# The order of emission of a fused attention and feed-forward kernel, rewritten from the thirtieth microsecond on

## The chip, the core and the metric

The kernel runs on one core of a Trainium2 chip. The metric is the device time of one execution in microseconds. Times of engines and waits come from one profiled execution. The five engines are TensorE (PE; PEld is its weight load), VectorE (DVE), ScalarE (ACT), GpSimd (POOL) and SyncE (SP), which here issues most DMAs. Each engine works through its own instructions in the order in which the program emitted them, and waits at the head of its queue until what the instruction needs is there.

## The reference

```python
# x (8, 8, 512, 64), state (8, 8, 32, 64): batch, head, token, depth
scores = x @ state.T / sqrt(D);   xread = softmax(scores) @ state      # tokens read the states
scores2 = state @ x.T / sqrt(D);  sread = softmax(scores2) @ x         # states read the tokens
x = concatenate([xread, sread], axis=2), heads side by side            # (8, 544, 512)
h = maximum(x @ w_in, 0)                                               # 512 -> 1024
conv_out = sum over k of conv_w[k] * h shifted by k - 1 along the tokens
out = (h * sigmoid(conv_out)) @ w_out                                  # 1024 -> 512
```

Everything is float32.

## The kernel before

The eight batches are taken one after the other, and the 1024 columns of the middle layer in eight slices of 128. A batch and a slice make a step `i = 8 b + f`, 64 steps in all. The 512 tokens of a batch lie on the free axis in a step; the 32 state tokens of four batches at a time are a side job of eight slices each (`ss`, `gts`, `acc_t` in the names).

Before its steps a batch needs the attention: `scores` on TensorE, softmax both ways on ScalarE and VectorE (`top`, `exp2`, `flip`, `read` for the states; `att_flip` to `att_low` for the tokens), and `state_product`, which multiplies the states by `w_in` at once, so that the first layer of a step is attention weights `a` times `u`. Products that must be exact to float32 are made of three passes of a high and a low part (`PASSES`): a value is split by `high` on ScalarE (L205) and `low` on VectorE (L208).

One step is this chain: `hidden` (six matmuls into `ps_h`, L630), `relu` (ScalarE L200 or VectorE L202, into `h`), `middle` (the middle tap, ScalarE L194 or VectorE L196, into `t`), `before` and `behind` (the other two taps, VectorE L673 and L678), `sigmoid` (a tanh on ScalarE, L682), `gate` (VectorE L687), `gate_high` (ScalarE L205, `g0`), `gate_low` (VectorE L208, `g1`), and then four times `project` (three matmuls each, L705), one for each 128 tokens, which add the slice to one of four accumulators `acc`. After eight steps `end` (L719, L721) copies an accumulator out of PSUM and `store` writes it. `join` and `edge` (GpSimd, L648) copy one column each between `h` and the state tokens' `hs`: `behind` reads what `join` has written, and the side job what `edge` has.

Weights arrive as `raw` and are rounded and split first (`w_abs` to `w_low`; `whole` and `wo` are `w_out`'s). Buffers are few: eight PSUM banks, five of `h`, five of `t`, four of `g0` and of `g1`, one of `xx` (the tokens for `read`), four of `xt`.

All operations are first entered in a list with what they read and write, in program order; `Plan.order` then emits them in the order of the numbers in `ORDER`. A number with a `v` puts the operation on VectorE instead of ScalarE, and `-n` emits n idle matmuls. Nothing else sets the order. It may be any that respects the reads and writes:

```python
        for word in ORDER.split():
            i = int(word.rstrip("v"))
            ...
            assert after[i] <= done and i not in done, "an operation before one that it needs"
            fns.append(partial(self.ops[i][2], on=self.vector) if word[-1] == "v" else self.ops[i][2])
```

Of the kernel before, what the change touches and what calls it, by code (L numbers as in the profile page):

```python
# [61 lines left out]
199 191 43 515 490 44 535 491 45 47 193 46 202 203 48 205 516 493 204 517 49 536 206 502 503 210 504 519v 494 537 520  # L62
# [12 lines left out]
228 662 607 611 229 639 706 691 690 656 623 638 1661 721 676v 663 654 707 677 664 665 424 678 666 340 425 719 689 692  # L75
# [14 lines left out]
447 938 448 967 1027 1030 482 473 953 1029 980 474 483 485 997 400 401 1045v 402 1031 475 968 476 484 941 999 1015 478  # L90
# [6 lines left out]
1068 1139 1124 1080 1140 1173v 1094 1108 1067 1070 1095 1174 1081 1096 1157 1109 1083 1143 1082 374 1172 1097 1171  # L97
1142 1141 1069 1175 1176 1089 1110 1085 1098 1100 1111 1159 1125 375 377 1084 1112 1144 376 378 1126 1104 1156 1116
1160 1161 1128 1177 409 1129 1199 1184 1117 1543 991 1145 1200 1185 1130 1544 1186 1187 1127 1545 1178 1131 1546 1132
1548 1133 1099 1214 1229 1549 1188v 1162 1550 1230v 1134 1114 1120 1163 1146 1551 1121 1552 1539 1215 1553 1113 1115  # L100
1118 1547 1252 1216 1189 1147 1164 1554 1122v 415 418 1148 416 417 1137 1149 1218 1297 1135 1282 1150 1179 449 1556
1557 1136 1165 419 1558 1219 1233v 1253v 1190 1220 1123 1119 1256 1203 1204 1231 1201 1191 1217 1152 1555 1167 1182
1151 1221 1192 1138 1180 1193 1559 1298v 1234 1235 1202 1232 1254 1194 1257 1205 1258 1560 1561 1236 1206 1153 1312
1301v 1168 1166 1181 1222 1562 1237 1207 1267 1195 1183 1313v 1197 1198 1259 1208 1563 1342 1223 1209 1210 1224 1283
1302 1299 1255 1564 1268 1271 1238 1565 1566 1272 1269 1273 1213 1239 1274 1212 1227 1225 1567 1568 1275 1569 1196
1211 1285 1300 1284 1570 1286 1270 1343v 1346v 1572 1287 1573 1347 1574 1288 1228 1226 1241 1243 1575 1240 1289 1246
1260 1250v 1576 1357 450 1327 1242 1358v 1577 1578 1303 1276 1261 1304 1571 1579 451 1247 452 1262 1277 1290 456 1328v
1316v 1248v 1249 453 454 1265 1291 455 1305 1263 1306 1280 1585 1251 1380 1381 459 1315 1580 1345 1383 457 1382 1344
1317 1307 1292 1278 1384v 1586 1244 1314 1245 1385 1587 1361 460 1318 1331 1359 1319 1362 1363 1320 1266 1295 1264
1410 1281 1293 1364 1386 1411 1588 1589 1348 1365 1321 1590 1591 1279 1296 1308 1294 1322 458 1311 1395 1387 1388 1332  # L110
1396 1326 1397 1329 1330 1593 1366 1398 1309 1399v 1470 1594 1323 1455 1310 1349 1350 1595 1596 1333 1597 1456v 1413
1334 1335 1425 1598 1351 1599 1352 1601 1602 1400 1592 1485 1324 1600 1426 1427 1457 1336 1428 1360 1337 1603 1401
1458 1412 1604 1605 1471 1402 1606 1607 1609 1610 1459v 1414 1440 1341 1339 1325 1611 1612 1415 1367 1416 1613 1614
# [5 lines left out]
1479 1376v 1377 1453 1468 1469 1452 1645 1480 1646 1647 1648 1494 1649 1650 1373 1652 1651 1495 1467 1483 1484 1466  # L119
1482 1497 1653 1499 1506 1507 1514 1515 1504v 1505 1512 1513 1498 1510 1508 1511 1509 1481 1496 1500 1502 1501 1503  # L120
"""


class Plan:

# [825 lines left out]
```

## Time and profile before

| | |
|---|---|
| three runs | 356.61 us median, 355.37 to 356.98 |
| span of the profiled execution | 354.1 us, 2.5 under the median of the runs |
| TensorE | 348.6 us, 98%; weight loads 271.8 us, 77% |
| VectorE | 316.1 us, 89% |
| ScalarE | 256.1 us, 72% |
| GpSimd | 29.4 us, 8% |
| chain that ended last | 97% on TensorE |
| read from HBM, written | 25.71 MB, 8.91 MB |

A busy share is an average over the whole span: the windows say where an engine has room. The chain that ended last is followed back from the last instruction; each step of it goes to what released an instruction, or to the one before it on its engine. A chain that lies on one engine nearly all the time says that this engine was waited for, and did not wait. Durations of one instruction overlap those of the next one on the same engine, so starts tell more than sums of durations.

### The profile page before, as it was taken

To read this page: it belongs to the slowest core of one execution; us is meant where nothing else is said; L and a number is where in the kernel's file an instruction comes from. 1 tells how busy PE (TensorE), PEld (TensorE's weight loads), DVE (VectorE), ACT (ScalarE), POOL (GpSimd) and SP (SyncE) were. 2 spreads that over 40 slices of the span, in tenths; PEclk is the share of its full clock that TensorE was granted. 3 is DMA by queue.
4 is the path that set the end of the run, shared out by engine and by line. 5 is a ranking of instruction groups with operands and counts; after the bars stand their busy time and mean duration, and the time that the engine had idled before them with its cause. 6 is when DMAs were issued, how large, how long until landed. Compare 5 with 4: busy or idle time off the path is not lost.

```text
span 354.1 us, 6694 instructions
## 1 busy us (share of the span) xinstructions
PE 348.6 (98%) x2538; PEld 271.8 (77%) x2538; DVE 316.1 (89%) x563; ACT 256.1 (72%) x560; POOL 29.4 (8%) x90
## 2 busy tenths in 40 slices
PE   7999999999999999999999999999999999999995
PEld 6766758876788868878789887878788868888884
DVE  1999999999999999999999999987799898889950
ACT  3999999998777997859856657774745447548642
POOL 1000000010000000100000300042201001113000
PEclk9999999999999999999999999999999999999999
DMA  7989998201600033030400000001200011000205
GB/s 255 396 309 377 328 357 302 62 1 50 219 0 2 0 127 142 3 119 32 180 30 2 0 31 31 30 3 60 89 2 0 0 71 65 2 2 0 74 33 176
DMA packets 13584, 35.06 MB, mean 99 GB/s; under 512 B 1520, under 2 KB 4720, under 8 KB 12528
## 3 DMA queue, kind: packets, MB, share of 16 engines
q1 hardware_dynamic: 12976, 34.28, 27.1%
q8 instruction: 20, 0.33, 0.4%
q10 hardware_dynamic: 576, 0.35, 0.3%
q14 instruction: 12, 0.10, 0.1%
HBM read 25.71 MB, written 8.91 MB: 98 GB/s over the span
## 4 chain that ended last, share of the span: by engine, by line
PE 97%; DMA 2%; ACT 0%; SPq 0%; issue 0%
PE acc L705 47%; PE ps_h L630 22%; PE ps_h L637 4%; PE ps_hs L615 4%; PE ps_u L548 4%; PE acc_t L705 3%; PE ps_r L368 2%; PE ps_t L355 2%; PE ps_s L310 2%; DMA xt<-xT 2%; PE acc_c L705 2%; PE acc L713 2%; PE ps_u L567 1%; PE ps_s L498 1%; PE ps_x L498 1%; PE ps_x L512 1%
## 5 line engine op out<-in xcount | busy, mean ns | idle before, releaser
L705 PE MATMUL acc<-wo,g 128*128 128x512 f32 x726 | 177.0, 393 | 0.0
L705 PEld LDWEIGHTS acc<-wo,g 128*128 128x128 f32 x726 | 134.7, 188 | 32.8 <-issue 1.7
L630 PE MATMUL ps_h<-a,u 128*128 128x512 f32 x336 | 83.2, 391 | 0.0
L630 PEld LDWEIGHTS ps_h<-a,u 128*128 128x128 f32 x336 | 62.7, 188 | 13.1
L682 ACT ACTIVATE t<-t 128x512 f32<-128x512 f32 x64 | 39.9, 630 | 14.5 <-DVE t L678 14.3
L673 DVE SCALAR_TENSOR_TENSOR t<-h,cw,t 128x511 f32<-128x511 f32 x64 | 47.1, 742 | 1.6 <-ACT t L194 1.5
L678 DVE SCALAR_TENSOR_TENSOR t<-h,cw,t 128x512 f32<-128x512 f32 (+1 forms) x64 | 46.8, 745 | 0.6
L205 ACT ACTIVATE g<-t 128x512 fp32r<-128x512 f32 (+1 forms) x62 | 37.5, 615 | 11.0 <-DVE t L687 5.5
L687 DVE SCALAR_TENSOR_TENSOR t<-t,h 128x512 f32<-128x512 f32 (+1 forms) x64 | 42.4, 667 | 2.3 <-ACT t L682 2.2
L208 DVE TENSOR_TENSOR g<-t,g 128x512 fp32r<-128x512 f32 (+1 forms) x62 | 41.3, 671 | 3.5 <-ACT g L205 3.1
L194 ACT ACTIVATE t<-h,cw 128x512 f32<-128x512 f32 x52 | 36.9, 723 | 4.3 <-DVE h L202 3.0
L200 ACT ACTIVATE h<-ps_h 128x512 f32<-128x512 f32 x56 | 33.3, 596 | 9.3 <-PE ps_h L630 6.1
L648 POOL COPY h<-hs 128x1 f32<-128x1 f32 x40 | 14.2, 376 | 129.2 <-ACT sr L383 66.3
L205 ACT ACTIVATE u<-ps_u 128x512 fp32r<-128x512 f32 x28 | 16.2, 596 | 8.5 <-PE ps_u L548 8.5
L719 ACT ACTIVATE o<-acc 128x512 f32<-128x512 f32 (+1 forms) x30 | 15.8, 544 | 8.5 <-PE acc L705 8.3
L648 POOL COPY hs<-h 128x1 f32<-128x1 f32 x40 | 13.6, 361 | 97.6 <-ACT h L200 80.9
L208 DVE TENSOR_TENSOR u<-ps_u,u 128x512 fp32r<-128x512 f32 x28 | 18.6, 682 | 2.5 <-ACT u L205 2.5
L615 PEld LDWEIGHTS ps_hs<-sr,wi 128*128 128x128 f32 x128 | 14.8, 192 | 1.1 <-ACT t L194 0.8
L637 PE MATMUL ps_h<-p,u 128*128 128x256 f32 x64 | 15.3, 386 | 0.0
L615 PE MATMUL ps_hs<-sr,wi 128*128 128x128 f32 x128 | 15.0, 276 | 0.0
L548 PE MATMUL ps_u<-wi,st 64*32 64x512 f32 x224 | 14.3, 597 | 0.0
L637 PEld LDWEIGHTS ps_h<-p,u 128*128 128x128 f32 x64 | 11.6, 190 | 3.3 <-DVE hc L249 0.8
(99 smaller groups left out, 400.3 us busy)
## 6 DMA issues: line engine op xcount, KB each, us to landing
xt<-xT SPq DMA_DIRECT2D x16, 512.0 KB, 7.7
xx<-xn SPq DMA_DIRECT2D x8, 1024.0 KB, 5.9
out<-o SPq DMA_DIRECT2D x27, 256.0 KB, 2.1
raw<-w_in SPq DMA_DIRECT2D x8, 512.0 KB, 7.6
raw<-w_out SPq DMA_DIRECT2D x8, 512.0 KB, 7.4
out<-o SPq DMA_DIRECT2D x6, 128.0 KB, 1.8
out<-o_t SPq DMA_DIRECT2D x8, 64.0 KB, 1.7
st<-stT SPq DMA_DIRECT2D x1, 448.0 KB, 10.2
```

The lines of the kernel that those rows point to most:

```text
L194: A.activation(dst, src, AF.Copy, scale=scale)
L200: A.activation(dst, src, AF.Relu, scale=0.5)
L205: A.activation(hi, src, AF.Copy)
L208: engine.tensor_tensor(lo, src, hi.bitcast(F32), op=ALU.subtract)
L615: PE.matmul(ps_hs[m, f][:, :NT], wi[:, k, f * P:(f + 1) * P], sr[m][:, k, :], start=(k == 0), stop=(k == NK - 1))
L630: PE.matmul(ps_h[i], u[j][:, g, fs], a[k][:, g, :], start=(n == 0), stop=(n == 3 * NG - 1))
L637: PE.matmul(ps_h[f][:, q * HS:(q + 1) * HS], us[0, f // 4][0][:, g, f % 4 * P:(f % 4 + 1) * P], half_of(pa[0], q)[:, g, :], start=(g == 0) ...
L673: V.scalar_tensor_tensor(t[:, 1:], h[:, :S - 1], cw[:, f, 0:1], t[:, 1:], op0=ALU.mult, op1=ALU.add)
L678: V.scalar_tensor_tensor(t[:, :n], h[:, 1:n + 1], cw[:, f, 2:3], t[:, :n], op0=ALU.mult, op1=ALU.add)
L682: A.activation(tt[i], tt[i], AF.Tanh, scale=0.25)
L687: V.scalar_tensor_tensor(tt[i][:, :n], tt[i][:, :n], 1.0, hd[i][:, :n], op0=ALU.add, op1=ALU.mult)
L705: PE.matmul(acc, g[j][:, cs], wo[:, k, f, :], start=(f == 0 and n == 0), stop=(f == NF - 1 and n == 2))
```

## The change

`ORDER` alone is new, from its 146th word on; what comes before (the first thirty microseconds) is the same. The new list has the same numbers. Of the `v` marks, 21 stand instead of 25: three `relu` instead of eight are on VectorE, thirteen `middle` instead of twelve, and five `end` in either. One line of the list as it was and as it is:

```diff
-211 122 137 212 470 471 472 538 521 159 158 208 161 213 506 545 575 546 138 162 214 163 134 507 560 207 56 50 51 139
+211 122 137 212 470 471 472 538 521 159 158 134 495 50 506 507 138 207 533 208 508 209 213 214 161 139 162 163 169 62
```

VectorE where the low part of step 6 (`g1_6`) is made, about 77 us into the run. Before:

```order
L208 TENSOR_TENSOR u1_1_1_1072<-ps_u_1_1_1_1074,u0_1_1_1071 128x512
L208 TENSOR_TENSOR u1_1_1_1072<-ps_u_1_1_0_1073,u0_1_1_1071 128x512
L340 TENSOR_REDUCE nm2_11_1130<-at_5_922 128x1
L690 SCALAR_TENSOR_TENSOR last_88<-t_7_997,h_7_871 128x128
L678 SCALAR_TENSOR_TENSOR t_8_1042<-h_8_1038,cw_78,t_8_1042 128x512
L690 SCALAR_TENSOR_TENSOR last_88<-t_6_909,h_6_896 128x128
L208 TENSOR_TENSOR g1_6_1137<-t_6_909,g0_6_1136 128x384
```

The same place now (`whole_6` is a slice of `w_out`, `hc_15` part of the rounding of another):

```order
L260 SCALAR_TENSOR_TENSOR whole_6_1040<-raw_14_885,hc_14_996 128x512
L673 SCALAR_TENSOR_TENSOR t_7_1008<-h_7_821,cw_78,t_7_1008 128x511
L249 TENSOR_SCALAR hc_15_1044<-hc_15_1044 128x512
L687 SCALAR_TENSOR_TENSOR t_6_914<-t_6_914,h_6_893 128x384
L690 SCALAR_TENSOR_TENSOR last_88<-t_5_959,h_5_671 128x128
L208 TENSOR_TENSOR wo_80<-whole_6_1040,wo_80 128x512
L208 TENSOR_TENSOR g1_6_1080<-t_6_914,g0_6_1079 128x384
```

Taps of step 8 and the low parts of batch 1's state product stood ahead of `g1_6` and now stand behind it; the weights' own low part moved ahead of it.

VectorE around step 48 (the first of batch 6). Before:

```order
L678 SCALAR_TENSOR_TENSOR t_47_3125<-h_47_3014,cw_78,t_47_3125 128x512
L208 TENSOR_TENSOR g1_44_3167<-t_44_3010,g0_44_3166 128x512
L673 SCALAR_TENSOR_TENSOR t_48_3133<-h_48_3127,cw_78,t_48_3133 128x511
L678 SCALAR_TENSOR_TENSOR t_45_3135<-h_45_2969,cw_78,t_45_3135 128x512
L678 SCALAR_TENSOR_TENSOR t_48_3133<-h_48_3127,cw_78,t_48_3133 128x512
L756 SCALAR_TENSOR_TENSOR ss_0_5_3112<-ss_0_5_3112,hs_83 128x128
L196 TENSOR_SCALAR t_51_3197<-h_51_3170,cw_78 128x512
L687 SCALAR_TENSOR_TENSOR t_46_3085<-t_46_3085,h_46_3032 128x512
```

Now:

```order
L208 TENSOR_TENSOR g1_47_3227<-t_47_3191,g0_47_3226 128x512
L196 TENSOR_SCALAR t_48_3239<-h_48_3233,cw_78 128x512
L756 SCALAR_TENSOR_TENSOR ss_0_7_3199<-ss_0_7_3199,hs_83 128x128
L673 SCALAR_TENSOR_TENSOR t_48_3239<-h_48_3233,cw_78,t_48_3239 128x511
L678 SCALAR_TENSOR_TENSOR t_48_3239<-h_48_3233,cw_78,t_48_3239 128x512
L208 TENSOR_TENSOR gts1_0_7_3243<-ss_0_7_3199,gts0_0_7_3242 128x128
L687 SCALAR_TENSOR_TENSOR t_48_3239<-t_48_3239,h_48_3233 128x512
L202 TENSOR_SCALAR h_49_3267<-ps_h_49_3249 128x512
L208 TENSOR_TENSOR g1_48_3265<-t_48_3239,g0_48_3264 128x512
L673 SCALAR_TENSOR_TENSOR t_49_3286<-h_49_3267,cw_78,t_49_3286 128x511
```

Four or five steps were under way on VectorE at a time; now one step runs from its middle tap to its low part before the next one's taps begin.

TensorE where it first reads `g1_48`. Before (`ps_h_48` was made some 140 rows of the list earlier):

```order
L548 MATMUL ps_u_7_1_0_3398<-wi_79,st_81 32x512
L548 MATMUL ps_u_7_1_1_3399<-wi_79,st_81 32x512
L705 MATMUL acc_6_2_3417<-wo_80,g1_48_3370 128x512
L705 MATMUL acc_6_2_3417<-wo_80,g0_48_3369 128x512 x2
L705 MATMUL acc_6_0_3426<-wo_80,g1_48_3370 128x512
L705 MATMUL acc_6_0_3426<-wo_80,g0_48_3369 128x512 x2
```

Now (the last row of `ps_h_48` stands 14 rows ahead of the first of these):

```order
L630 MATMUL ps_h_49_3249<-a0_6_2674,u0_6_0_2731 128x512
L705 MATMUL acc_t_0_2196<-wo_80,gts1_0_7_3243 128x512
L705 MATMUL acc_t_0_2196<-wo_80,gts0_0_7_3242 128x512 x2
L705 MATMUL acc_5_3_2976<-wo_80,g1_47_3227 128x512
L705 MATMUL acc_5_3_2976<-wo_80,g0_47_3226 128x512 x2
L705 MATMUL acc_5_2_2969<-wo_80,g1_47_3227 128x512
L705 MATMUL acc_5_2_2969<-wo_80,g0_47_3226 128x512 x2
L705 MATMUL acc_6_3_3273<-wo_80,g1_48_3265 128x512
L705 MATMUL acc_6_3_3273<-wo_80,g0_48_3264 128x512 x2
```

Between `hidden(48)` and its first product stood `hidden` of later steps and products of earlier ones; now four products of steps 45 to 47, `hidden(49)`, one product of the state tokens and two of step 47 do.

## Rows read from the trace of the kernel before

**Rows 1.** Windows: us, then PE, PEld, DVE, ACT, POOL busy (instructions), clock, DMA.

```profile
32.00:73.00 41.00, 40.96 (x448) 29.68 (x447) 39.59 (x79) 39.45 (x97) 1.65 (x2) 1.00 0.71 259
130.00:240.00 110.00, 110.00 (x807) 87.98 (x796) 106.36 (x170) 79.69 (x166) 12.35 (x39) 1.00 0.15 53
240.00:354.00 114.00, 110.53 (x521) 88.91 (x519) 90.01 (x172) 63.60 (x134) 14.07 (x41) 1.00 0.13 44
```

**Rows 2.** Chain that ended last: start, us on the chain, engine, tile, line, count.

```profile
71.00 1.02 PE ps_u L548 x16
...
86.02 1.88 PE ps_u L548 x32
...
315.83 8.84 PE acc L705 x39
```

**Rows 3.** The profile's first line: busy us, share of the span, instructions.

```profile
PE 348.6 (98%) x2538; PEld 271.8 (77%) x2538; DVE 316.1 (89%) x563; ACT 256.1 (72%) x560; POOL 29.4 (8%) x90
```

**Rows 4.** Groups by line and shape: count, busy us, mean ns, idle before.

```profile
L630 PE MATMUL ps_h<-a,u 128*128 128x512 f32 x336 | 83.2, 391 | 0.0
...
L673 DVE SCALAR_TENSOR_TENSOR t<-h,cw,t 128x511 f32<-128x511 f32 x64 | 47.1, 742 | 1.6 <-ACT t L194 1.5
L678 DVE SCALAR_TENSOR_TENSOR t<-h,cw,t 128x512 f32<-128x512 f32 x56 | 41.0, 745 | 0.6
L208 DVE TENSOR_TENSOR g<-t,g 128x512 fp32r<-128x512 f32 x56 | 37.9, 684 | 3.5 <-ACT g L205 3.1
L687 DVE SCALAR_TENSOR_TENSOR t<-t,h 128x512 f32<-128x512 f32 x56 | 37.9, 683 | 2.3 <-ACT t L682 2.2
L196 DVE TENSOR_SCALAR t<-h,cw 128x512 f32<-128x512 f32 x12 | 5.8, 482 | 0.7 <-ACT h L200 0.6
...
L682 ACT ACTIVATE t<-t 128x512 f32<-128x512 f32 x64 | 39.9, 630 | 14.5 <-DVE t L678 14.3
L205 ACT ACTIVATE g<-t 128x512 fp32r<-128x512 f32 x56 | 34.5, 625 | 11.0 <-DVE t L687 5.5 <-PE acc L705 5.1 <-DVE t L673 0.2
L200 ACT ACTIVATE h<-ps_h 128x512 f32<-128x512 f32 x56 | 33.3, 596 | 9.3 <-PE ps_h L630 6.1 <-DVE t L687 3.0
```

**Rows 5.** Timeline, step 49 at 273 us: start, us, engine, line, operation, count.

```profile
273.08 0.58 ACT L200 ACTIVATE h<-ps_h 128x512 f32<-128x512 f32 x1
273.70 0.72 ACT L194 ACTIVATE t<-h,cw 128x512 f32<-128x512 f32 x1
...
274.45 0.75 DVE L673 SCALAR_TENSOR_TENSOR t<-h,cw,t 128x511 f32<-128x511 f32 x1
275.31 0.75 DVE L678 SCALAR_TENSOR_TENSOR t<-h,cw,t 128x512 f32<-128x512 f32 x1
...
276.10 0.63 ACT L682 ACTIVATE t<-t 128x512 f32<-128x512 f32 x1 [1.15 <-DVE t L678]
```

**Rows 6.** Timeline, low parts and first products of steps 4 and 6.

```profile
63.88 0.56 DVE L208 TENSOR_TENSOR g<-t,g 128x384 fp32r<-128x384 f32 x1
...
70.16 0.84 PE L705 MATMUL acc<-wo,g 128*128 128x512 f32 x3
...
76.68 0.56 DVE L208 TENSOR_TENSOR g<-t,g 128x384 fp32r<-128x384 f32 x1
...
80.42 1.52 PE L705 MATMUL acc<-wo,g 128*128 128x512 f32 x6
```

**Rows 7.** Timeline, the end of the run: last matmuls and last copies.

```profile
343.57 6.96 PE L705 MATMUL acc<-wo,g 128*128 128x512 f32 x30
...
350.57 0.66 ACT L719 ACTIVATE o<-acc 128x256 f32<-128x256 f32 x2 [0.70 <-PE acc L705]
```

**Rows 8.** Timeline, GpSimd's copies beside VectorE.

```profile
149.34 0.54 POOL L648 COPY hs<-h 128x1 f32<-128x1 f32 x4
...
196.18 0.75 DVE L673 SCALAR_TENSOR_TENSOR t<-h,cw,t 128x511 f32<-128x511 f32 x1
196.24 0.72 POOL L648 COPY hs<-h 128x1 f32<-128x1 f32 x1
```

More of the change, by code (lines that the diff above doesn't have):

```diff
@@ L62 @@
 199 191 43 515 490 44 535 491 45 47 193 46 202 203 48 205 516 493 204 517 49 536 206 502 503 210 504 519v 494 537 520
[12 rows of a table removed]
-228 662 607 611 229 639 706 691 690 656 623 638 1661 721 676v 663 654 707 677 664 665 424 678 666 340 425 719 689 692
[14 rows of a table removed]
-447 938 448 967 1027 1030 482 473 953 1029 980 474 483 485 997 400 401 1045v 402 1031 475 968 476 484 941 999 1015 478
[6 rows of a table removed]
-1068 1139 1124 1080 1140 1173v 1094 1108 1067 1070 1095 1174 1081 1096 1157 1109 1083 1143 1082 374 1172 1097 1171
-1142 1141 1069 1175 1176 1089 1110 1085 1098 1100 1111 1159 1125 375 377 1084 1112 1144 376 378 1126 1104 1156 1116
@@ L99 @@
[L99 to L113, printed above, removed]
[5 rows of a table removed]
@@ L119 @@
-1479 1376v 1377 1453 1468 1469 1452 1645 1480 1646 1647 1648 1494 1649 1650 1373 1652 1651 1495 1467 1483 1484 1466
-1482 1497 1653 1499 1506 1507 1514 1515 1504v 1505 1512 1513 1498 1510 1508 1511 1509 1481 1496 1500 1502 1501 1503
[16 rows of a table added]
+756 263 757 785 778 815 759 760 786 789v 264 761 845 790 800 816 819 820 779 780 762 763 830 308 801 265 787 385 791
[18 rows of a table added]
+1085 1107 368 1089 1100 373 1124 1044 1564 1565 1108 1109 1110 1125 1127 1098 1111 1115 1114 1120 1126 1566 1128v 1129
+1130 1113 1122v 1131 1132 1112 1133 1139 1140 412 1154 1134 1136 1137 1104 414 1121 1138 1143 1169 1118 1155 1119 1144
@@ new lines @@
+1141 1145 1567 1568 1158v 1146 374 1147 1148 1156 1159 1170 1160 1161 1149 1135 1150 1151 377 375 1173v 1162 376 1152
+1163 1164 1171 1059 1174 1175 1153 1168 1166 1123 1167 1172 1165 1569 1570 378 1184 1176 1177 1178 1179 1181 409 1185
+1199 1186 1116 1188v 1189 1190 1200 1203v 1191 1192 1204 1183 1187 1193 1194 1180 1214 1215 1201 1205 1218 1216 1219
+1206 1220 1221 1182 1571 1198 1202 1196 1207 1222 1208 1117 1197 1223 1195 1229 1230 1209 1210 1224 1225 1211 1233v
+1226 1232 1234 1231 1572 1213 1573 1574 1228 1252 1212 1227 1235 1236 1575 1237 1238 1239 1240 1253 1255 1241 1256v
@@ new lines @@
+1576 1577 1254 1257 1258 1578 1267 1579 1243 1259 1260 1261 1268v 1242 1262 1266 1264 1269 1263 1271 1250 1251 1248
+1282 1265 1272 1273 1249 1274 1275 1276 1277 1244 1283 1284 1286v 1287 1288 1289 1270 1281 1279 1278 1297 1157 1217
+1246v 1290 1280 1291 1285 1298v 1301 1247 415 416 1292 1293 1295 1294 418 1302 1299 1303 1304 1142 419 1296 417 1312
+1305 1327 449 450 1306 1307 1310 1309 1308 1311 1313 1316v 1328 1329 1314 1317 1318 1585 1331 1319 1332 1320 1321 1315
+1245 1333 1334 1342 1343 1580 1322 1335 1336 1337 1357 1326 1325 1340 1346v 1344 1347 1586 1348 1358 1361 1362 1349
[3 rows of a table added]
@@ new lines @@
+1410 1411 1412 1413 1405 1391 1414v 1415 1416 1601 1372 1600 1392 1407 1408 1409 1425 1373 1417 1602 1603 1604 1418
+1605 1419 1406 1420 1424 1422 1421 1423 1606 1607 1608 1378 1426 1428 1440 1609 1379 1610 1300 1611 1455 1429 1430
+1612 1427 1613 1614 1431 1615 1432 1433 1376v 1584 1377 1581 1617 1618 1434 1616 1435 1439 1437 1441 1330 1442 1443
+1619 1444 1438 1436 1445 1620 1456 1459 1621 1446 1622 1460 1623 1447 1448 1625 1626 1457 1461 1449 1450 1462 1360
+1458 1627 1624 1628 1463 1464 1470 1471v 1472 1629 1474 1630 1465 1485 1453 1468 1475 1631 1632 1476 1486 1489 1490
@@ L121 @@
+1633 1634 1452 1451 1477 1478 1487 1491 1479 1492 1454 1469 1480 1467 1483 1484 1493 1494 1582 1473 1482 1635 1636
+1637 1495 1488 1638 1639 1641 1642 1643 1499 1514 1644 1515 1497 1645 1646 1512 1647 1513 1498 1510v 1504 1640 1505
+1511 1506 1507 1648 1649 1508v 1650 1509 1653 1466 1651 1481 1652 1496 1502 1500 1501 1503
 """
```

72 rows, old and new, of the table ORDER are left out of this document.

## The prediction

> **What bounds the kernel now.** I read the windows first, then the chain of waits, then the groups of instructions by line, and last the timeline at the few places where the new order is tight. The windows show TensorE busy in 40.96 of 41.00 us from 32 to 73 us and in all of the 110 us from 130 to 240 [rows 1]; only the last window has idle time, and that is the drain. In the same rows VectorE is busy 39.59 of 41 us and ScalarE 39.45 of 41 early on, VectorE 106.36 of 110 in the middle, and 90.01 of 114 at the end. So TensorE is the bound from 32 us to its last matmul, VectorE is close behind it until about 240 us, and ScalarE too until 73 us.
>
> A busy TensorE could hide pauses, because its matmuls overlap: each is drawn 391 ns long [rows 4], but the chain of waits shows 39 of them in 8.84 us, one per 0.227 us [rows 2]. Groups of three (one `project`, 0.68 us) and of six (one `hidden`, 1.36 us) follow each other at that rate almost everywhere.
>
> **The change, part by part.** No instruction is added, and the arithmetic is the same; the sequence is. What moves:
>
> *TensorE's own work: 0, between -0.2 and +0.2 us.* The groups are the same, and what they cost depends on neighbours only where the short 64-row groups stand: one group of 16 takes 1.02 us, two together 1.88 us [rows 2]. The old order has five such neighbours and the new one six: 0.16 us gained, which one more change between kinds of matmul can take back. The page of the profile has matmuls busy in 98% of the span and weight loads in 77% [rows 3], so the room that is counted depends on which of the two is read; the even 0.227 us say that what weight loads leave free isn't time in which another matmul could start.
>
> The Trainium skill, "Perfetto Trace Analysis", section "Identifying the Most-Contended Engine", says that matmul busy time is a bad measure of TensorE's headroom and that the busy share of weight loads is a better one. By that rule an order could still find up to 21% of the span, some 74 us, and the sum would start from a gain; by the rows it starts from 0, and I go by the rows.
>
> *A shorter distance between `hidden(i)` and the first `project(i)`.* In the old order some 140 rows of TensorE's list lie between them for step 48, in the new one 20: four groups of three, `hidden(49)`, and three more groups of three, 7 x 0.68 + 1.36 = 6.12 us. From step 40 on all 24 distances are 5.9 to 11.5 us, seven of them (40, 44, 46, 48, 49, 50, 58) at most 6.2. Before, TensorE never came near its operand: the distances were 20 us and more. Now the chain through ScalarE and VectorE must fit, and I add it up from the means [rows 4]: the last matmul ends 0.391 - 0.227 = 0.16 us after its slot; relu 0.596; middle tap on VectorE 0.482; the two other taps 0.742 and 0.745; tanh 0.630; gate 0.683; the high part 0.625; the low part 0.684. That is 5.19 of work and 5.35 with the matmul's end. A hand-over is 0.03 us: relu ends at 273.66 and the middle tap starts at 273.70, the second tap ends at 276.06 and tanh starts at 276.10 [rows 5]; nine of them are 0.27. Between the two taps the same rows have 0.11 (275.20 to 275.31), so 0.08 more. The next weights must load one matmul ahead, 0.23. Together 5.93 us; with the middle tap on ScalarE (0.72 [rows 5]) 6.17.
>
> Step 48 has 6.12 for 5.93, less 0.09 for a small side instruction that stands between its taps: it just fits, with 0.1 to spare. Step 49 doesn't: its relu is on VectorE behind `gate(48)`, its middle tap on ScalarE behind `gate_high(48)`. If step 48 is ready at 5.79 us (from the end of `hidden(48)`), gate(48) ended at 4.42, relu(49) runs 4.34 to 5.03, and the middle tap 5.06 to 5.78, the taps to 7.41, tanh to 8.07, gate to 8.78, high to 9.44, low to 10.15. TensorE wants the first operand at 6.12 + 6 x 0.68 = 10.20 (`hidden(50)` counted as two) less 0.26: 9.94. It waits 0.2 us. I take six waits of this size for the seven tight steps: 1.2 us; bounds 0 (if each chain is 0.2 shorter) and 7 (24 steps by 0.3).
>
> *The stretch from 33 to 73 us: 0.6 us.* Here I go from the old trace and count differences. The old order starts `project(4)` at 70.16 and `project(6)` at 80.42; its low parts end at 63.88 + 0.56 = 64.44 and 76.68 + 0.56 = 77.24 [rows 6]. In the new order three `hidden` (4.08) and one `state_hidden` (0.9) no longer stand ahead of `project(4)`: TensorE is there at 65.2. VectorE has two taps fewer ahead of the low part and four small steps more, +0.4 by my count: 64.8. For `project(6)` five `hidden` (6.8) leave: 73.6. On VectorE three taps, a gate, two low parts of the state product and some small ones leave (4.9) and two come (0.9): 73.3. So where the old order had 5.7 and 3.2 us to spare, the new one has 0.3 to 0.4, and the weight load takes 0.26 of that. These sums hold VectorE's old idle time, 41.00 - 39.59 = 1.41 us [rows 1], within them. As ScalarE has only 1.55 us to spare there, each tenth that VectorE loses more is a tenth for TensorE. I take 0.6, about half of what it loses now, between 0 and 1.4.
>
> *73 to 240 us: 0.4 us.* Distances of 6.9 to 8.3 us stand at steps 28, 29 and 31, where wide softmax instructions of one microsecond on ScalarE and 1.2 on VectorE stand in the same queues. I worked step 29 through by hand with those and came to a wait of about half a microsecond; the other steps have room. Bounds 0 and 2.
>
> *The end: 0.3 us.* `hidden(62)` and `hidden(63)` now stand eight and eleven groups ahead of their first products (6.8 and 7.5 us), and `gate_low(63)` stands behind side work of the state tokens, so that its operand is 0.2 to 0.4 late. The drain after the last matmul, from 350.5 to the span's end at 354.1, keeps its length: two copies of 0.33 us and a store [rows 7]. The two copies change places, which I cost at 0, within 0.3 either way. Loads keep their order but for a few; the only one that comes close is the load for `read(1)`, cost 0, at most 0.5.
>
> *Sum.* 0 + 1.2 + 0.6 + 0.4 + 0.3 = 2.5 us on a span of 354.1: 356.6. The three runs have a median of 356.61, 2.5 over the profiled span; with that, 359.1 us, +0.7%. What a measurement of this kernel tells from no change is about 0.5%, 1.8 us.
>
> **The rivals.** *No change: the margins hold.* In the last third VectorE is busy in only 79% [rows 1]. If the two taps meet with 0.03 between them instead of 0.11, and instructions of other steps fall into the pauses rather than ahead of the chain, 5.93 becomes 5.85 and a step like 49 regains most of its 0.2. Then the tight steps from 40 on, and the end, cost nothing, and what is left is the early 0.6 or less: 356.6 to 357.6, centre 357.1. It decides at a chain of about 5.9 us. For it speaks that hardly one of the 24 distances lies under 5.93; against it that margins of 0.1 us must hold seven times, with other steps' instructions in the same queues.
>
> *Much slower: GpSimd's copies.* Each step needs one copy of a column (`join`, `h<-hs`) before its second tap, and one back. Alone they are quick, four in 0.54 us beside a reduction; beside a two-input instruction of VectorE one took 0.72, and ended with that instruction, at 196.96 and 196.93 [rows 8]. In the old order no tap waited for long, as relu was far ahead. In the new one a second tap comes 1.3 us after relu, with the copy and up to four others in GpSimd's queue. If half of the last 24 steps lose one such hold, 0.5 us each, that is 6 us on top of about 1 elsewhere: 363.6. Against it: a waiting VectorE frees the copy, which then takes 0.18.
>
> The Trainium skill, "SBUF — State Buffer", section "SBUF: two separate sides", states the lock behind this: a VectorE instruction with two SBUF inputs and a GpSimd instruction that reads SBUF exclude each other for the whole instruction. This trace agrees at 196.24 us, as above.
>
> *Faster.* It would take a TensorE that now waits, or a shorter drain. The first has 0.04 us in the window of 32 to 73 [rows 1], and the drain can give 0.3; room inside TensorE's busy time would have to lie in the 0.227 us, which is the same everywhere: 353.8 at best for the span, 356.3 for the runs. Only chance in the measurement would show more than 0.5%.
>
> **How the numbers follow.** Small waits as summed: 0.50, with its own range of 357.6 to 361.5. No change: 0.32. GpSimd's holds: 0.12. Faster: 0.06. A fifth of the first case (0.10) lies within 0.5%. So faster 0.06, same 0.41 (0.32 less 0.01, and 0.10), slower 0.53. The predicted time is that of the first case, 359.1. The range reaches from 356.3, which leaves out the fast end of no change and the faster case, to 363.0, which takes in the first case and a mild form of the holds.
>
> **What would show it.** Right: TensorE with waits on `acc<-wo,g` released by VectorE's `g` (L208), none over 0.6 us, between 33 and 73 us and again from 230 us on; its busy time and count as before; VectorE's busy total as before, its idle time moved to the middle. The holds would show as second taps (L678) that wait for GpSimd. Wrong would be a TensorE with no waits of more than 0.1 us after 32 us; waits above 1 us at single places (a load, a buffer that comes free late), which no term here has; or a drain that differs by more than 0.5 us.

## The result, and the profile after

The changed kernel takes 359.2 us (median of 19 runs; 359.1 without one that took 708, the others 358.0 to 361.8) against 356.76 us for the kernel before (19 runs, 355.37 to 359.24). The ratio is 1.0070, with a 95% interval of 1.0050 to 1.0091: 2.5 us slower. Its profiled execution took 359.56 us with a span of 357.8, 3.7 more than the 354.1 before. In all runs the time lies 1.7 to 1.8 us above the span, so the profile before is of an execution of some 355.9 us, 0.9 under the median. A profile shows one execution, which can be some us longer or shorter than the median, and the times of those below are given with them.

The first line of the page of the changed kernel answers to [rows 3]; below it the shares of its chain by engine.

```profile
PE 351.2 (98%) x2538; PEld 271.5 (76%) x2538; DVE 319.0 (89%) x559; ACT 264.0 (74%) x564; POOL 23.9 (7%) x90
...
PE 95%; DMA 4%; SPq 0%; issue 0%; ACT 0%
```

TensorE's count is the same and its share is the same; the chain now has 4% of DMA where it had 2%. The windows of the changed kernel, columns as in [rows 1], the last one to its own end:

```profile
32.00:73.00 41.00, 39.75 (x446) 28.58 (x439) 38.16 (x76) 38.23 (x95) 0.39 (x1) 0.95 0.69 246
130.00:240.00 110.00, 110.00 (x830) 87.47 (x829) 106.84 (x175) 80.42 (x172) 8.27 (x30) 0.95 0.13 49
240.00:358.00 118.00, 114.23 (x542) 89.04 (x540) 94.57 (x168) 71.82 (x138) 13.43 (x50) 0.95 0.12 41
```

From 32 to 73 us TensorE had 0.04 us idle and now has 1.25. The view of waits (engine, tile, line, releaser: total, times, longest) says what that is; the kernel before has no such line:

```profile
PE ps_r L368 <- DMA xx<-xn: 1.3, 1, 1.3
```

It is one wait, at `read(3)`, for its load of tokens. The timeline of the changed kernel around it, first SyncE's issues, then TensorE (start, us, engine, line, operation, count):

```profile
44.89 0.33 SPq L298 DMA_DIRECT2D xt<-xT  x1
45.97 0.33 SPq L302 DMA_DIRECT2D xx<-xn  x1
46.35 0.53 SPq L298 DMA_DIRECT2D xt<-xT  x1
...
43.74 1.13 PE L310 MATMUL ps_s<-xt,st 64*32 64x512 f32 x16
44.80 1.11 PE L368 MATMUL ps_r<-xx,e2t 128*32 128x64 f32 x64
...
51.52 1.28 PE L705 MATMUL acc<-wo,g 128*128 128x512 f32 x3
54.05 1.11 PE L368 MATMUL ps_r<-xx,e2t 128*32 128x64 f32 x64 [1.25 <-DMA xx<-xn]
```

The same in the kernel before:

```profile
44.54 0.33 SPq L302 DMA_DIRECT2D xx<-xn  x1
44.92 0.94 SPq L298 DMA_DIRECT2D xt<-xT  x2
...
43.39 1.10 PE L368 MATMUL ps_r<-xx,e2t 128*32 128x64 f32 x64
...
51.29 1.09 PE L310 MATMUL ps_s<-xt,st 64*32 64x512 f32 x16
52.31 0.88 PE L368 MATMUL ps_r<-xx,e2t 128*32 128x64 f32 x48
```

There is one `xx` buffer, and the reads come in the order 2, 1, 3, so the load for `read(3)` is issued when `read(1)` is done with it. Before, 7.77 us lay between issue and read, and that was enough. Now `read(1)` itself is 1.4 us later (44.80 against 43.39), half a megabyte more (`xt(10)`) stands ahead in the queue, and `scores(4)`, one microsecond of work, has gone behind `read(3)`: TensorE wants the tokens at 52.63, 6.66 us after issue, and gets them after 8.08.

Where the 3.7 us are: 1.4 at this load (the start of `read(3)` is 1.42 us behind its slot); 1.2 in twelve short losses of 0.05 to 0.17 us between matmuls, ten of them behind 250 us (where starts lie more than 0.227 us apart, leaving out the 0.09 to 0.11 where TensorE changes from one kind of matmul to another, which the old order has too, 25 times from 57 us on); about 1.2 in matmuls with plain float32, which in this execution, with a granted clock of 0.95 throughout, took 617 ns where before they took 597 (1.2 is what the same operations take less in the profile of the first experiment). The last is the execution's, not the order's: other runs of the changed kernel at a clock of 1.0 have spans from 356.2 us. Without it the profiles differ by some 2.5 us, as the timed runs do, and both lie some 0.8 to 0.9 us under their medians.

The small waits are drawn at TensorE's weight loads. In the view of waits of the weight loads from 240 us on, the changed kernel has

```profile
PEld acc L705 <- DVE g L208: 2.6, 7, 0.9
```

and the kernel before has none released by `g`. It has

```profile
PEld acc L705 <- DVE o L721: 1.7, 2, 0.8
```

and no start behind them that is late. So a weight load can wait up to 0.8 us ahead of its matmul without any loss, and most of the 2.6 us cost nothing; what is lost shows in the matmuls. At step 58 of the changed kernel:

```profile
326.85 0.64 PEld L705 LDWEIGHTS acc<-wo,g 128*128 128x128 f32 x3
...
327.08 2.27 PE L705 MATMUL acc<-wo,g 128*128 128x512 f32 x8
327.18 0.69 DVE L208 TENSOR_TENSOR g<-t,g 128x512 fp32r<-128x512 f32 x1 [0.50 <-ACT g L205]
...
327.92 1.22 PEld L705 LDWEIGHTS acc<-wo,g 128*128 128x128 f32 x6 [0.43 <-DVE g L208]
```

The low part ends at 327.87, the load of it starts 0.05 later, and eight matmuls take 2.27 us where 7 x 0.227 + 0.394 = 1.98 is the rule: 0.29 lost, the largest place (0.17 ahead of the first matmul of step 58 and 0.11 behind it).

### The profile page after: what moved, and what is told of

Its sections match the earlier page's. It is cut to its first block, busy times and chain, and to the rows that moved or that the text cites. A ratio compares the mean times of both kernels' runs of the same rounds, so it can differ in the third digit from the quotient of the medians.

```text
span 357.8 us, 6714 instructions
## 1 busy us (share of the span) xinstructions
PE 351.2 (98%) x2538; PEld 271.5 (76%) x2538; DVE 319.0 (89%) x559; ACT 264.0 (74%) x564; POOL 23.9 (7%) x90
## 4 chain that ended last, share of the span: by engine, by line
PE 95%; DMA 4%; SPq 0%; issue 0%; ACT 0%
PE acc L705 46%; PE ps_h L630 21%; PE ps_h L637 4%; PE ps_hs L615 4%; PE ps_u L548 4%; PE acc_t L705 3%; PE ps_r L368 2%; DMA xx<-xn 2%; PE ps_t L355 2%; PE ps_s L310 2%; DMA xt<-xT 2%; PE acc_c L705 2%; PE ps_u L567 1%; PE ps_s L498 1%; PE ps_x L498 1%; PE ps_x L512 1%
## 5 line engine op out<-in xcount | busy, mean ns | idle before, releaser
L630 PE MATMUL ps_h<-a,u 128*128 128x512 f32 x336 | 81.9, 390 | 0.0
L205 ACT ACTIVATE g<-t 128x512 fp32r<-128x512 f32 (+1 forms) x62 | 38.5, 622 | 20.7 <-DVE t L687 20.0
L200 ACT ACTIVATE h<-ps_h 128x512 f32<-128x512 f32 x61 | 36.2, 595 | 16.9 <-PE ps_h L630 16.5
L648 POOL COPY hs<-h 128x1 f32<-128x1 f32 x40 | 10.1, 264 | 148.9 <-ACT h L200 116.1
```

The costliest lines, as they stand in the source:

```text
L200: A.activation(dst, src, AF.Relu, scale=0.5)
L205: A.activation(hi, src, AF.Copy)
L630: PE.matmul(ps_h[i], u[j][:, g, fs], a[k][:, g, :], start=(n == 0), stop=(n == 3 * NG - 1))
```

## The experiments

Each run stands beside runs of the kernel before on the same chip; 0.1% is 0.36 us. Theory A: the load costs 1.4 and the short distances about 0.8. Theory B: the prediction's own terms. Theory C: TensorE's work itself became dearer.

**The load first.** `xt(10)` is 338, the load for `read(3)` 242.

```diff
-246 251 180 338 109 247 252 492 525 526 181 242 339
+246 251 180 109 247 252 492 525 526 181 242 338 339
```

> The new order with one move: SyncE issues the load of the tokens for read(3) (1 MB) ahead of the load xt(10) (512 KB) that stood one place before it. In the changed kernel's profile TensorE waits 1.42 us for that load at 52.4 us, the only wait above 0.2 us. Theory A (that load costs 1.4 us and the short distances from step 40 on about 0.8): the 1 MB stand behind 0.5 MB less, some 1.2 us of the 16 engines' time, so the wait shrinks to 0.0 to 0.4 us and the time to about 358.0 (before 356.8, changed 359.2). Theory B (the prediction's sum: 0.6 for VectorE's margins from 33 to 73 us, 0.4 in the middle, 1.2 from step 40 on, 0.3 at the end, loads nothing in most executions): 359.2, no difference, and the waits stand elsewhere. Theory C (TensorE's own work became dearer, by its neighbours or by the granted clock of 0.949): 359.2 too.

358.73 us, 1.0054 (1.0037 to 1.0071): 0.6 less than the changed kernel, whose 1.0070 lies within that interval, so the time alone decides for no theory. Its profile (an execution of 357.41 us) has 0.73 instead of 1.42 at `read(3)`, 7.21 us after issue. That points A's way, at half A's size. The Trainium skill, "DMA: Bandwidth & Descriptors", section "Two DMAs through the same engine are not ordered", says that descriptors of one queue on one DMA engine start in order. The traces agree as far as they go: in the four profiles with the 0.5 MB ahead (changed kernel, new order to 58 us, `hidden` earlier and later) `read(3)` began 7.84 to 8.67 us after the issue of its load, later than here.

**New order to 58 us only, and old order to 58 us only.** The seam is at the 300th operation (`att_back(1)`), where the two orders have done the same work but for six operations each.

```diff
-ORDER = new
+ORDER = new[:300] + rest of old        # in short; and the other way round
```

> The first 300 operations in the new order (to about 58 us), the rest in the old one; at the seam the two orders differ by twelve operations. Theory A: the load's wait of 1.4 us at read(3) is in it, nothing else: before plus 1.4, about 358.2. Theory B: about half of the 0.6 us of the early stretch, 357.1. Theory C: at most 0.3 more than before.

> The first 300 operations in the old order (to about 58 us), the rest in the new one. Theory A: no wait at read(3), the small waits from 250 us on as in the changed kernel: 0.8 above before, 357.6. Theory B: 2.2 above before, 359.0. Theory C: 359.2 less the share of the first 58 us, about 358.8.

The new beginning alone: 357.83 us, 1.0033 (1.0012 to 1.0054), 1.2 above before. The new rest alone: 357.99 us, 1.0036 (1.0016 to 1.0055), 1.3 above. The halves add up to the whole 2.5: the loss is in two places, of about the same size. B's 2.2 for the rest lies outside the interval, its 0.3 for the beginning too; so do C's 2.0 (barely) and 0.3. The profile of the first (an execution of 360.97 us) has 2.20 us lost at `read(3)`; that of the second (357.13) has no wait at a load.

**`hidden` earlier.** For twenty of the last 24 steps, as here 58 (1410) ahead of a product (1371) and a side instruction:

```diff
-1402 1403 1404 1371 1599 1410 1411
+1402 1403 1404 1410 1371 1599 1411
```

> The new order with hidden(i) of twenty of the steps 40 to 63 one group of TensorE earlier (0.68 us more between hidden(i) and its first product; steps 40, 44, 52 and 53 stay). Theory A: the waits of 0.05 to 0.2 us at steps 41, 46, 49, 57 and 58 go, the load's 1.4 us stays: 0.6 to 0.8 less than the changed kernel, 358.5. Theory B: 1.2 less, 358.0. Theory C: 359.2.

358.19 us, 1.0035 (1.0013 to 1.0057): 1.25 less than the changed kernel. That is B's 1.2; the interval holds A's 0.7 too. In its profile (357.71 us) the waits from 268 us on are gone, but `hidden(56)`, moved ahead of its own operand, loses 0.6; the load keeps its 1.37.

**`hidden` later.** The same move the other way (49 is 1267).

```diff
-1257 1258 1578 1267 1579 1243
+1257 1258 1578 1579 1267 1243
```

> The new order with hidden(i) of the steps 40 to 63 one group of TensorE later (0.68 us less to the first product where it follows directly): seven steps then have 5.0 to 5.4 us, five have 6.1. Theory A (the chain after hidden is 5.8 us long, from the trace of the changed kernel: 5.55 from the start of relu to the end of the low part, 0.16 of the last matmul, 0.1 for two hand-overs): waits of about 0.4 us at steps 40, 44, 46, 48, 49 and 58 and 0.8 at step 50, 3.2 in all, so 362.4 (bounds 361.5 to 363.3). Theory B (the prediction's chain of 5.93 to 6.17): waits of 0.5 to 0.7 and of 1.0, and 0.1 at the steps with 6.1: about 4.7 in all, 363.9. Theory C (the short distances have nothing to do with it): 359.2.

369.74 us, 1.0381 (1.0345 to 1.0417): 10.5 to 11.1 us more than the changed kernel, over twice what either theory gave. The view of waits of this kernel from 240 us on:

```profile
PE acc L705 <- DVE g L208: 4.1, 7, 1.3
PE acc_t L705 <- DVE gts L208: 2.5, 3, 1.4
PE acc L705 <- ACT h L200: 0.7, 1, 0.7
```

My error was to give slack to the steps with longer distances. The chain is 5.55 us only where a step has VectorE for itself; where two share it, it takes 6.5 to 8.3, as at steps 41 to 43 and 45. In the changed kernel's trace the low part ends 0.05 to 0.65 us ahead of its first product at 19 of the last 24 steps. And the edit took more than was meant: of the 24 distances twelve became one group shorter (0.68 us), those of steps 43 and 54 two, that of step 45 three. In its trace the starts of the matmuls from 240 us on lose 11.6 us against the even 0.227, where the changed kernel's lose 1.05; that accounts for the difference. So the order was tight nearly everywhere, not at seven steps.

**The load covered.** As the first experiment, `read(3)` (256) behind `scores(4)` (300), and `read_flip(3)` behind `project(3,0)`:

```diff
-514 529 80 256 300 505
+514 529 80 300 256 505
```

> The new order with the load for read(3) ahead of xt(10), and scores(4) on TensorE ahead of read(3) as in the old order, so that 1.0 us of work lies over the load; read_flip(3) goes behind project(3,0). Theory A: the load's wait is gone, only the small waits from 250 us on are left: 1.4 less than the changed kernel, 357.8, and no run with a mean granted clock of 0.995 or less. Theory B and C: 359.2.

358.68 us, 1.0043 (1.0026 to 1.0061): only 0.9 less, and a clock of 0.995 in one of ten runs. That one, of 361.2 us, is the profiled one, and in it the wait is at `read(1)`:

```profile
PE ps_r L368 <- DMA xx<-xn: 1.9, 1, 1.9
```

So the load for `read(1)` is short of time too, in some executions: in this one it was read 7.5 us after issue, in the changed kernel's profile 5.7 us after. The same with `hidden` earlier, as above but for step 56:

> Both repairs at once: the load for read(3) covered, and hidden(i) of nineteen of the steps 41 to 63 one group earlier. Theory A: load 1.4 and short distances 0.9 are all that the new order costs: 0.0 to 0.3 above before, 357.1 where before is 356.9. If something else in the new order costs time (more changes between kinds of matmul, VectorE's margins), 357.5 or more.

357.88 us, 1.0031 (1.0013 to 1.0049), where A had 357.1. Its profile (an execution of 359.7 us) has 1.5 us lost at `read(1)` and 0.6 behind `read(3)`. A covers the place but not the cause, as I now read it: three loads pass through one buffer, and `read(2)` stands 2.3 us later in the new order (37.95 against 35.69) and pushes the other two together. The load for `read(1)`, first in the kernel before and then in the changed one, is issued 2.2 us later,

```profile
36.89 0.33 SPq L302 DMA_DIRECT2D xx<-xn  x1
39.11 0.33 SPq L302 DMA_DIRECT2D xx<-xn  x1
```

but `read(1)` only 1.4: 5.7 us are left between them where there were 6.5.

**The reads earlier.** `read(2)` (215) two groups earlier, its load (201) ahead, `read(1)` (174) one group earlier, and the load first as above:

```diff
-575 590 591 141 576 201 56 54 165 215 172
+201 575 590 215 591 141 576 56 54 165 172
...
-160 243 244 245 68 297 298 60 166 174 499
+160 174 243 244 245 68 297 298 60 166 499
```

> The new order with read(2) two groups earlier (its load moved ahead with it), read(1) one group earlier, and the load for read(3) ahead of xt(10). In profiles of kernels with the new order's beginning TensorE waited at read(1) or at read(3), 0.7 to 2.5 us, and where read(3) was covered alone the wait stood at read(1). Theory A, mended: each load now has about the time that it had in the old order, the waits at both reads go (0.3 at most), no run shows a mean clock of 0.995 or less, and the time is 1.2 less than the changed kernel's, 358.0. If the loads are slow for another reason: no less than 358.7.

358.69 us, 1.0044 (1.0026 to 1.0062): 0.9 less, and the clock is 1.0 in all eight runs. That lies between the two expectations, and the interval holds both. Its profile (an execution of 359.36 us) still has waits at two reads and one at a `read_flip`:

```profile
PE ps_r L368 <- ACT wo L205: 0.9, 1, 0.9
PE ps_r L368 <- DMA xx<-xn: 0.6, 1, 0.6
PE ps_f L379 <- ACT rr L375: 0.6, 1, 0.6
```

The first, at `read(1)`, is put down to ScalarE, but it is the load's too: it landed at 45.13, 7.1 us after its issue, and the read began at 45.26. The third, at `read_flip(1)`, stands in the two profiles with the reads earlier and in no other, so the edit brings a cost of its own.

**Both causes taken away**: `hidden` earlier as above (but for step 56), once on top of the old beginning and once on top of the reads earlier:

> The first 300 operations in the old order (to about 58 us, so the three loads of tokens and their reads stand as before), the rest in the new order with hidden(i) of nineteen of the steps 41 to 63 one group earlier. Theory A, mended (the reads of the tokens stand too close to each other for one buffer, and the distances from step 40 on are just too short): nothing is left of the loss, before plus 0.0 to 0.4, 357.1 where before is 357.0. If something else in the new order costs time: 357.8 or more.

> The edits of the run before (reads earlier) and hidden(i) of nineteen of the steps 41 to 63 one group earlier: the new order with both repairs. Theory A, mended: before plus 0.0 to 0.4, 357.1 where before is 357.0. If something else in the new order costs time: 357.8 or more.

357.64 us, 1.0009 (0.9992 to 1.0027), and 357.41 us, 1.0012 (0.9993 to 1.0030), where before has 357.37: no difference that can be measured. Whatever else in the new order costs or gains time is under 1.0 us by these intervals. The reads earlier took 0.0026 off the ratio of the changed kernel and 0.0023 off that of `hidden` earlier. Each difference alone is within its margin, some 0.0028 from the two intervals; their mean, 0.9 us with some 0.7 either way, is not.

The first of the two profiles (357.85 us) shows that the old beginning has such waits as well, here 1.4 us at `read(2)`:

```profile
PE ps_r L368 <- DMA xx<-xn: 1.4, 1, 1.4
```

In the profile of the second (357.37 us) the waits at reads and at `read_flip(1)` are

```profile
PE ps_f L379 <- ACT rr L375: 0.6, 1, 0.6
PE ps_r L368 <- ACT h L200: 0.5, 1, 0.5
PE ps_r L368 <- DMA xx<-xn: 0.2, 1, 0.2
```

The second line is the load for `read(1)` again: it landed at 43.77, and the read began at 43.91. Loads and reads stand here as in the run before, so that the waits are shorter than its 0.9 and 0.6 is a difference between executions.

No version that beats the kernel before came of it.

**The load last**, behind `xt(11)` (339) and a load of weights (74):

```diff
-526 181 242 339 69
+526 181 339 69
...
-183 74 110
+183 74 242 110
```

> The new order with the load for read(3) issued behind xt(11) and one load of weights too, 1 MB more ahead of it in the queue. The runs of the changed kernel have a mean granted clock of 0.994 to 0.995 in three of eighteen, and one profile with a pause of 2 us at this place shows the clock at 0.61 in the four microseconds behind it. Theory A (the wait is the queue's data; the pause alone is paid): the wait grows by 1.0 to 1.3 us for each 0.5 MB, to 3.4 to 4.0 us, and the time to 361.5. Theory D (a long pause also brings the clock down behind it): another 1.9 us in most runs, 363.4, and the profile shows a stretch behind the pause at half the clock. Theory C: 359.2.

363.49 us, 1.0181 (1.0160 to 1.0203), 4.0 to 4.3 above the changed kernel. The pause grew to 4.25 us, 2.83 more, for 1 MB; against the four profiles named above, which lost 1.37 to 2.20 at this read, it is 2.0 to 2.9. From the start of `read(3)` to the first `state_hidden` it then takes 6.75 us, in the changed kernel 5.24, and 5.15 with `hidden` earlier and with `hidden` later, where the clock there was 1.00. The 1.5 us more are the clock's. Windows of this kernel (columns as in [rows 1]; the granted clock is the third from the end):

```profile
40.00:52.00 12.00, 12.00 (x120) 7.30 (x119) 11.40 (x25) 12.00 (x29) 0.00 (x0) 1.00 0.94 344
52.00:56.60 4.60, 0.52 (x7) 0.11 (x6) 4.57 (x10) 1.31 (x4) 0.00 (x0) 1.00 0.86 358
56.60:60.40 3.80, 3.80 (x88) 2.03 (x96) 0.60 (x1) 1.20 (x4) 0.00 (x0) 0.55 0.02 8
60.40:73.00 12.60, 12.60 (x97) 10.75 (x81) 9.90 (x16) 12.26 (x30) 0.00 (x0) 1.00 0.57 168
```

TensorE was busy at 1.00, idle 4.1 us, then busy 3.8 us at 0.55, nearly all of it the lower level of 1.2 GHz, then at 1.00 again. Theory D holds, with 1.5 for its 1.9.

## Why the prediction was right, and where it was not

The time, 359.2 against 359.1, was right, but half of that is luck: of the 2.5 us some 1.25 are the small waits of the likeliest case, and 1.2 come from a term that the sum had at 0. Two errors of opposite sign hid each other.

*TensorE's own work, 0 +- 0.2:* right. The two kernels without either cause are within 0.12% of before, and from 57 us on the 14 stretches of other kinds of matmul in the new order (in the profile with the old beginning) cost 0.1 us less than the old one's 24. So the forecast went by the right reading of the even 0.227 us: orders with 76% of weight loads found no room.

*Short distances, 1.2, and the end, 0.3:* the mechanism was right, the place nearly. Waits of 0.05 to 0.17 us, none over 0.6, add up to 1.05 in the trace from 240 us on, 0.89 of it at `acc<-wo,g` behind VectorE's `g` and the rest at a `hidden` and a product of the state tokens, and taking them away gave 1.25 (changed kernel to hidden earlier) and 1.15 (reads earlier to both). Step 49 waited 0.14 where 0.2 was worked out. The chain, 5.48 from relu to the low part by the means of [rows 4, 5] and seven hand-overs, took 5.55 where a step has VectorE for itself; only the hand-over to TensorE was cheaper, 0.05 and 0.11 for my 0.26. What I had wrong is which steps are tight: not seven, but most of the 24, as the later `hidden` showed.

*33 to 73 us, 0.6:* there was nothing. My margins, 0.3 to 0.4, were measured as 0.38 at step 4 and 0.49 at step 6 with the old beginning, where no load had given VectorE time. The step that failed is the one behind them: I charged half of VectorE's idle time although both margins cover the hand-over. In the changed kernel's own timeline:

```profile
65.76 0.55 DVE L208 TENSOR_TENSOR g<-t,g 128x384 fp32r<-128x384 f32 x1
...
66.96 1.29 PE L705 MATMUL acc<-wo,g 128*128 128x512 f32 x5
...
74.11 0.54 DVE L208 TENSOR_TENSOR g<-t,g 128x384 fp32r<-128x384 f32 x1
...
75.48 1.75 PE L705 MATMUL acc<-wo,g 128*128 128x512 f32 x7
```

Against [rows 6] the products are 3.2 and 4.9 us earlier, and the operands 0.65 and 0.83 ahead. Worked out were 65.2 and 73.6 us, and with the old beginning they start at 65.35 and 73.81; the rest is the lateness that the new beginning brings. The sign named for VectorE, idle time that moves to the middle, didn't come either: from 130 to 240 us it has 3.16 us of it against 3.64, from 32 to 73 us 2.84 against 1.41.

*73 to 240 us, 0.4:* 0.15, in two waits. Step 29 had 0.2 us to spare.

*Loads, 0, at most 0.5:* this is the step that failed most. "Loads keep their order but for a few; the only one that comes close is the load for `read(1)`": that compares orders of issue, not the time from the release of the one buffer to the read. The rows for it were there: in the old trace `read(1)` starts at 43.39, its successor's load is issued at 44.54, and 7.77 us later the read begins; the load had landed after 7.54. It cost 0.9 to 1.2 us in the runs (the reads earlier; the new beginning alone) and 1.4 in the profile. The text named a wait of more than 1 us at a single load as what would prove it wrong, and there it stands.

*Rivals.* No change was half right: margins of some tenths did hold from 33 to 240 us. GpSimd's holds didn't come: second taps waited for it 0.5 us in all, though 40 of the 64 read what a `join` on GpSimd wrote, with a mean of 359 ns.

```profile
L678 DVE SCALAR_TENSOR_TENSOR t<-h,cw,t 128x512 f32<-128x512 f32 (+1 forms) x64 | 47.3, 744 | 2.6 <-POOL h L648 0.5
L648 POOL COPY h<-hs 128x1 f32<-128x1 f32 x40 | 13.6, 359 | 97.0 <-ACT hs L646 65.8
```

*The drain* kept its length: the last two copies start 3.53 us ahead of the end, as in [rows 7].

```profile
354.27 0.66 ACT L719 ACTIVATE o<-acc 128x256 f32<-128x256 f32 x2 [1.39 <-PE acc L705]
```

Not settled: why the same load takes 5.7 us from issue to read in one execution and 7.5 in another. Waits at reads occur with the old beginning too (1.4 us in one of its three profiles), so the new order's loss there is a matter of how often, and a single profile can't size it. That the loads are the cause of the beginning's 1.2 us rests on the profiles, where from 32 to 58 us most of TensorE's waits are at reads, on the load put last, and on the reads earlier; no single edit of the loads gave back all of it.

## What to carry to other kernels

When an order of emission changes, follow every buffer that has only one copy: the time from its release (the read's end) through the queue to the next read is a distance like that between a matmul and its epilogue, and it shortens without any load changing places. Where the bound engine is never idle, a new order has little to win and can lose what each chain lacks of its distance; take the chain of each step with its neighbours on the queue, not the shortest one. And a sum that comes out right proves none of its terms: two hybrids at a seam where both orders have done the same work told in two runs where the loss lay.

## What the runs showed of the hardware

A pause of TensorE costs more than itself when the clock falls behind it, and pauses of the same length do not always bring that. A mean granted clock of 0.995 or less was seen in three of seventeen runs of the changed kernel beside the profiled one, in two of twelve with the new beginning alone, two of twelve with `hidden` earlier, one of four with `hidden` later, one of ten with the load covered, and all five with the load last; of 80 runs of the kernel before beside them one had it (0.994), and of the 68 of the other six kernels none. Those runs of the changed kernel took 360.8 to 361.8 us, some 2 us above its median; one more took 361.7 at 0.998. The Trainium skill, "TensorE: Matmul & The Clock Gate", section "HAM oscillation — how this bites in real kernels", describes this: a wait for a DMA lets the clock drop and the next work starts slowly. The trace agrees, at 0.55 behind 4.1 us of idle time, and the run whose profile showed 2.2 us of wait had 0.61 in the four microseconds behind it. But where 1.99 us were lost (load covered) the clock fell behind the read, and where 2.04 were lost (`hidden` later) it stayed at 1.00. The windows behind the read, in this order (columns as in [rows 1]):

```profile
56.00:60.00 4.00, 4.00 (x96) 1.46 (x85) 2.44 (x6) 2.09 (x5) 0.00 (x0) 0.61 0.36 133
46.00:50.00 4.00, 3.97 (x68) 2.64 (x69) 1.91 (x3) 2.17 (x8) 0.00 (x0) 0.57 0.69 230
54.00:58.00 4.00, 4.00 (x102) 2.44 (x103) 2.80 (x6) 2.82 (x9) 0.00 (x0) 1.00 0.57 215
```

In the one execution with a mean clock of 0.95 from end to end the plain float32 matmuls took 3 to 4% longer, and the others as long as before. Groups by shape, changed kernel first, then the one with the load first, whose clock was 1.00 (count, busy us, mean ns):

```profile
L705 PE MATMUL acc<-wo,g 128*128 128x512 f32 x726 | 176.2, 394 | 0.0
L548 PE MATMUL ps_u<-wi,st 64*32 64x512 f32 x224 | 14.8, 617 | 0.0
```

```profile
L705 PE MATMUL acc<-wo,g 128*128 128x512 f32 x726 | 176.1, 394 | 0.0
L548 PE MATMUL ps_u<-wi,st 64*32 64x512 f32 x224 | 14.3, 596 | 0.0
```

Ends of matmuls are modelled, but the starts say the same: the products are 0.227 us apart (median) in both. So at this clock the 0.227 us are set by something that a clock 5% lower doesn't slow; what it is, no run here shows.
